# Channel layers over row blocks of 512, 64+448, 448 and 128+128, and 256 and 320, with left rows carried to the next pass

## The chip, the cores and the metric

One NeuronCore of one Trainium2 chip runs the whole program. The metric is device time in microseconds of one execution; the median of three runs stands for the kernel.

## What is computed

Four batches of 576 tokens with 512 channels go through three layers:

- attention over 8 heads of 64, where scores below the row's maximum minus tau are dropped before the softmax;
- a mixing layer and the channel layers: `u = x + h` (h mixes the tokens through a rank of 32), then `u + relu(u @ w_ch1) @ w_ch2`, with 512 to 2048 to 512 channels and the same weights for every token;
- a mixture of 8 experts: a gate gives each token an expert (a local gate can keep the expert of the token before), and the token goes through that expert's two layers of 512 to 1024 to 512.

The channel layers treat each token (each row) by itself: any rows can share a pass over the weights.

## The kernel before

Activations are kept transposed: a tile `yT` holds 128 channels on the partitions, four such groups `d`, and the 576 rows of a batch along the free dimension. `X[b]` is that tile for batch b; two tiles alternate, so batch b+2 takes the tile of batch b.

The channel layers keep the precision of float32 by splitting each operand into a high and a low part (tiles ending in h and l) and adding three products: high by high, high by low, low by high. Each product is a matmul of TensorE, with a 128 by 128 block of weights held in the array and the rows as the moving operand.

- `mix(b)` (L583) splits the rows of batch b into `uh` and `ul`: ScalarE copies (L591), VectorE subtracts (L592), in 8 steps.
- `load_w(b, f)` (L598) fetches one of 16 slices f of both weight matrices from DRAM and splits it.
- `mlp_l1(b, f)` (L618) makes the hidden values of slice f. It goes over the rows in two blocks, `HALVES`, of 256 and 320. For each block twelve matmuls (L628 to L630, over four k) add up in one bank of PSUM; ScalarE takes the relu from it (L631), VectorE the low part (L632).
- `mlp_l2(b, f0)` (L636) multiplies four slices of hidden values by the second weights, again twelve matmuls for a block of rows and a group d (L645 to L647); VectorE adds the bank to `yT` (L648).
- `channel(b)` (L651) runs 16 slices of layer 1 and three of the four rounds of layer 2; `channel_end(b)` (L662) the last round and `logits(b)`: the gate's matmuls (L675), a copy (L676), six transposes (L683) and two reductions (L684).
- `store_rows(b)` (L688) transposes the rows back and writes them to DRAM; `route(b)` (L701) works out each token's expert and its rank among that expert's tokens with many small VectorE instructions and four small matmuls, one of them L737.

The PSUM banks of the channel layers come from `mm_tile` (L137), which has two. Attention has its own: two tiles for scores (`s`, L132) and two banks for transposes (`tp`). A score tile is filled by L293 and L295, read by VectorE for the maximum (L328), by ScalarE for the exponential (L339) and by VectorE for the mask (L343). The probabilities are transposed (L390), copied out (L391, L398) and multiplied by v (L409, L410, L413); a chain per head pair then normalises and mixes them, ending in L467.

The order of the work comes from `interleave` (L72), which takes the next piece of whichever generator is least far along; the second number of each pair is the total of the costs that its generator reports, and every block of the channel layers reports 1.5. A scheduler of the language then orders each engine's instructions by that order and by what is ready; it does not change the program's pieces. Attention of batch 0 runs alone with the conversion of the weights beside it. After it (L785) the attention of batch b runs beside the channel layers of batch b-1:

```python
    for b in range(1, B):
        interleave((attention(b), 65.0), (channel(b - 1), 82.0), (STORE.get(b - 2, iter(())), 15.0),
                   (route(b - 2), 5.0) if b > 1 else ((1.0 for _ in conv), 30.0))
        if b == 1:
            cvs.close()
        interleave((mix(b), 2.1), (channel_end(b - 1), 18.0))
        STORE[b - 1] = store_rows(b - 1)
```

The channel layers of the last batch run at L1183 beside `early_slots()` (L915): the stored rows and the routing of batch 2, then slots of two experts' first tokens (their indices are cast at L911), and the loads of the first expert's weights. The experts follow; their first rows are gathered at L1059. Their layer 1 is L1106 to L1108, their layer 2 L1151 to L1153, there with 512 columns of weights as the moving operand.

Of the kernel before, what the change touches and what calls it, by code (L numbers as in the profile page):

```python
# [8 lines left out]
F32 = mybir.dt.float32  # L9
# [21 lines left out]
CH = 96  # L31
# [52 lines left out]
def attention_channel_moe(ctx, tc, qk, vv, tau, umat, vrep, wch, wgl, wexp, consts, out):  # L84
# [52 lines left out]
    def mm_tile(name):  # L137

        NM[0] += 1
        if PX and TURN[0] and NM[0] % 3 == 0:  # L140
            return PX[0].tile([128, 512], F32, tag="l1", name=name, bufs=2)
        return MM[0].tile([128, 512], F32, tag="mm", name=name, bufs=2)
# [437 lines left out]
        while pend or CHAIN:  # L580
            piece()

    def mix(b):  # L583

        u = X[b]
        uh = mlp.tile([128, 4, S], F32R, tag="uh", name=f"uh{b}")
        ul = mlp.tile([128, 4, S], F32R, tag="ul", name=f"ul{b}")
        for o, n in HALVES:
            c = slice(o, o + n)
            for d in range(4):  # L590
                act.activation(uh[:, d, c], u[:, d, c], AF.Copy)  # L591
                dve.tensor_tensor(out=ul[:, d, c], in0=u[:, d, c], in1=uh[:, d, c].bitcast(F32), op=ALU.subtract)  # L592
                yield 0.15
        U[b] = (uh, ul, u)

    W, LAST = {}, []

# [17 lines left out]
            r.append((hi, lo))  # L615
        W[nm] = r

    def mlp_l1(b, f, hs):  # L618
        uh, ul, _ = U[b]
        (w1h, w1l), _ = W[f"{b}_{f}"]  # L620
        hh = mlp.tile([128, S], F32R, tag="hh", name=f"hh{b}_{f}", bufs=5)
        hl = mlp.tile([128, S], F32R, tag="hl", name=f"hl{b}_{f}", bufs=5)
        hs[f] = (hh, hl)
        for o, n in HALVES:
            pm = mm_tile(f"l1_{b}_{f}_{o}")[:, :n]
# [5 lines left out]
            act.activation(hh[:, o:o + n], pm, AF.Relu)  # L631
            dve.scalar_tensor_tensor(out=hl[:, o:o + n], in0=pm, scalar=0.0, in1=hh[:, o:o + n].bitcast(F32),  # L632
                                     op0=ALU.max, op1=ALU.subtract)
            yield 1.5

    def mlp_l2(b, f0, hs):  # L636
        yT = U[b][2]
        for d in range(4):
            wd = slice(d * 128, d * 128 + 128)
            for o, n in HALVES:  # L640
                pm = mm_tile(f"l2_{b}_{f0}_{d}_{o}")[:, :n]
                for f in range(f0, f0 + 4):
                    _, (w2h, w2l) = W[f"{b}_{f}"]
                    hh, hl = hs[f]
                    pe.matmul(pm, lhsT=w2h[:, wd], rhs=hh[:, o:o + n], start=(f == f0), stop=False)  # L645
                    pe.matmul(pm, lhsT=w2h[:, wd], rhs=hl[:, o:o + n], start=False, stop=False)  # L646
                    pe.matmul(pm, lhsT=w2l[:, wd], rhs=hh[:, o:o + n], start=False, stop=(f == f0 + 3))  # L647
                dve.tensor_tensor(out=yT[:, d, o:o + n], in0=pm, in1=yT[:, d, o:o + n], op=ALU.add)  # L648
                yield 1.5

    def channel(b):  # L651
        hs = {}
        load_w(b, 0)
        load_w(b, 1)
        for f in range(NF):
            yield from mlp_l1(b, f, hs)
            if f % 4 == 0 and f:
                yield from mlp_l2(b, f - 4, hs)
            load_w(b, f + 2)
        HS[b] = hs  # L660

    def channel_end(b):  # L662
        yield from mlp_l2(b, NF - 4, HS[b])
        yield from logits(b)

    HS, LG = {}, {}

    def logits(b):

        yT = U[b][2]  # L670
        lt = mlp.tile([128, S], F32, tag="yr", name=f"lt{b}", bufs=2)
        for o, n in HALVES:
            pl = mm_tile(f"lt{b}_{o}")
            for d in range(4):
                pe.matmul(pl[32 * d:32 * d + 32, :n], lhsT=wg_sb[:, d], rhs=yT[:, d, o:o + n], start=True, stop=True)  # L675
# [3 lines left out]
        L = LG[b] = mlp.tile([CH, NJ, 9], F32, tag="L", name=f"L{b}")  # L679
# [6 lines left out]
        yield 2.6  # L686

    def store_rows(b):  # L688

        yT = U[b][2]  # L690
        for c0 in range(0, S, 128):
            n = min(128, S - c0)
            py = px_tile("l2", f"py{b}_{c0}") if b == B - 2 else mm_tile(f"py{b}_{c0}")
            for d in range(4):
                pe.transpose(py[:n, d * 128:d * 128 + 128], yT[:, d, c0:c0 + n], ident)
            yr = mlp.tile([128, S], F32, tag="yr", name=f"yr{b}_{c0}", bufs=2)[:n, :DM]
            act.activation(yr, py[:n], AF.Copy)  # L697
            sp.dma_start(out=ydram[b * S + c0:b * S + c0 + n, :], in_=yr)
            yield 0.45

    def route(b):  # L701

        w = mlp
        rt_tile = (lambda n: px_tile("l1", n)) if b == B - 2 else mm_tile
# [482 lines left out]
    for _ in store_rows(B - 1):  # L1187
        pass
    for _ in route(B - 1):
        pass  # L1190
# [96 lines left out]
```

## Time and profile before

| what | value |
|---|---|
| median of 3 runs | 1058.18 us (1057.45 to 1060.41) |
| the profiled execution's own time | 1055.3 us |
| its span, from the first to the last instruction | 1053.5 us |
| mean granted clock of TensorE | 0.994 of full speed |

The profile is of one execution. Busy time of an engine is the time in which it has an instruction running; matmuls overlap in the records, so their start-to-start distances, not their durations, say what one costs. A few matmul records are missing. Engines are PE (TensorE's matmuls), PEld (its weight loads), DVE (VectorE), ACT (ScalarE), POOL (GpSimd) and SP (the queue of most transfers); a row of the windows gives the busy times in that order, POOL last, then the granted clock (PEclk), the DMA share and GB/s. A wait is idle time of an engine with what ended it. Stages are cut at the gate's matmuls (L675) that follow each batch's channel layers.

### The profile page before, as it was taken

The page shows a single profiled execution, that of the slowest core. Times are in us where ns is not written, and L with a number is a line of the kernel's source. Part 1 is how long each engine was busy: PE and PEld are TensorE (multiplying, and loading weights), DVE is VectorE, ACT ScalarE, POOL GpSimd, SP SyncE. Part 2 cuts the span into 40 slices and gives each one's busy share as a digit, 9 for nine tenths or more (in the row PEclk, how much of TensorE's full clock was granted, in tenths as well). Part 3 has the DMA queues.
Part 4 walks back from the last instruction along what each step waited for, and adds up shares of the span by engine and source line. Part 5 has one row for each costly group of instructions (what it writes and reads, how often), then busy time and mean ns, then how long its engine had stood idle before and what let it go on. Part 6 is the DMA issues. An engine that isn't in the chain of part 4 may idle for free. (4 is left out here: it accounts for less than half of the span.)

```text
span 1053.5 us, 19168 instructions
## 1 busy us (share of the span) xinstructions
PE 1014.9 (96%) x7083; PEld 897.4 (85%) x7084; DVE 706.6 (67%) x1709; ACT 570.2 (54%) x1216; POOL 134.6 (13%) x115
## 2 busy tenths in 40 slices
PE   7898999999999999999999999999999999999996
PEld 4666688898888999898989988999998988989984
DVE  7998676775777577576667655583367855566673
ACT  6888665674646466473646545432254344455462
POOL 1331132230100000000000000002420321111100
PEclk9999999999999999999999999999999999999998
DMA  6655577773423232141322101353145475456650
GB/s 213 217 155 153 151 227 237 246 228 108 133 70 104 66 101 86 57 132 57 105 77 66 51 31 61 112 194 107 54 151 180 151 265 170 150 187 208 204 180 15
DMA packets 59205, 143.80 MB, mean 136 GB/s; under 512 B 8349, under 2 KB 9117, under 8 KB 59104
## 3 DMA queue, kind: packets, MB, share of 16 engines
q1 hardware_dynamic: 55744, 132.28, 39.4%
q0 software_dynamic: 3360, 10.23, 3.0%
q8 instruction: 57, 0.93, 0.4%
q14 instruction: 44, 0.36, 0.1%
HBM read 124.65 MB, written 18.61 MB: 136 GB/s over the span
## 5 line engine op out<-in xcount | busy, mean ns | idle before, releaser
L628 PE MATMUL l<-uh,w0h 128*128 128x256 f32 (+1 forms) x512 | 159.1, 311 | 0.6 <-DVE L L684 0.2
L645 PE MATMUL l<-hh,w1h 128*128 128x256 f32 (+1 forms) x512 | 155.6, 304 | 0.0
L630 PE MATMUL l<-uh,w0l 128*128 128x256 f32 (+1 forms) x512 | 153.0, 299 | 0.0
L647 PE MATMUL l<-hh,w1l 128*128 128x256 f32 (+1 forms) x512 | 152.8, 299 | 0.0
L646 PE MATMUL l<-hl,w1h 128*128 128x256 f32 (+1 forms) x512 | 152.7, 298 | 0.0
L629 PE MATMUL l<-ul,w0h 128*128 128x256 f32 (+1 forms) x512 | 152.6, 298 | 0.0
L1037 ACT ACTIVATE eh<-ew 128x512 fp32r<-128x512 f32 x160 | 94.3, 628 | 71.8 <-PE el L1153 45.3
L1038 DVE TENSOR_TENSOR el<-ew,eh 128x512 fp32r<-128x512 f32 x160 | 106.7, 693 | 37.7 <-ACT eh L1037 36.3
L339 ACT ACTIVATE p<-s,st 128x576 f32<-128x576 f32 x144 | 104.5, 740 | 47.0 <-DVE st L328 46.2
L343 DVE SCALAR_TENSOR_TENSOR p<-s,st,p 128x576 f32<-128x576 f32 x144 | 114.2, 814 | 9.8 <-ACT p L339 6.2
L328 DVE TENSOR_REDUCE st<-s 128x1 f32<-128x576 f32 x144 | 105.1, 750 | 19.7 <-PE s L295 19.1
L391 ACT ACTIVATE ptt<-tp 128x512 f32<-128x512 f32 (+1 forms) x192 | 89.9, 495 | 41.2 <-PE tp L390 40.6
L648 DVE TENSOR_TENSOR yT<-l,yT 128x256 f32<-128x256 f32 (+1 forms) x128 | 58.3, 456 | 67.8 <-PE l L647 67.5
L293 PE MATMUL s<-kh,qs 128*128 128x288 f32 x320 | 95.1, 317 | 8.8 <-DVE p L343 6.8
L612 POOL TENSOR_TENSOR w1l<-wr,w1h 128x512 fp32r<-128x512 f32 x24 | 32.7, 1379 | 545.1 <-ACT w1h L610 534.3
L628 PEld LDWEIGHTS l<-uh,w0h 128*128 128x128 f32 x512 | 97.1, 190 | 4.3 <-ACT yr L697 1.7
L645 PEld LDWEIGHTS l<-hh,w1h 128*128 128x128 f32 x512 | 97.0, 189 | 2.5 <-DVE p L343 0.8
L390 PE MATMUL tp<-cst,p 128*128 128x128 f32 x576 | 90.0, 275 | 8.5 <-ACT ptt L391 8.2
L629 PEld LDWEIGHTS l<-ul,w0h 128*128 128x128 f32 x512 | 97.3, 190 | 0.5
L646 PEld LDWEIGHTS l<-hl,w1h 128*128 128x128 f32 x512 | 97.1, 190 | 0.6
L630 PEld LDWEIGHTS l<-uh,w0l 128*128 128x128 f32 x512 | 97.3, 190 | 0.1
L647 PEld LDWEIGHTS l<-hh,w1l 128*128 128x128 f32 x512 | 96.9, 189 | 0.2
(448 smaller groups left out, 2296.6 us busy)
## 6 DMA issues: line engine op xcount, KB each, us to landing
ew<-in_wexp_dram SPq DMA_DIRECT2D x80, 512.0 KB, 4.7
wr<-wdram SPq DMA_DIRECT2D x128, 256.0 KB, 2.9
cr<-in_wch_dram SPq DMA_DIRECT2D x32, 512.0 KB, 5.1
raw<-in_qk_dram SPq DMA_DIRECT2D x30, 304.0 KB, 3.2
wdram<-w SPq DMA_DIRECT2D x32, 256.0 KB, 2.8
v<-in_vv_dram SPq DMA_DIRECT2D x16, 352.0 KB, 3.6
raw<-in_qk_dram SPq DMA_DIRECT2D x16, 320.0 KB, 3.5
raw<-in_qk_dram SPq DMA_DIRECT2D x17, 288.0 KB, 3.5
```

What stands on the lines that cost most here:

```text
L293: pe.matmul(s["t"][:, h, :288], lhsT=qs[:, qc:qc + 128], rhs=kh[:, k0:k0 + 288], start=(j == 0), stop=False)
L328: dve.tensor_reduce(out=self.st[:, 0, h:h + 1], in_=self.t[h], axis=AX.XY, op=ALU.max, negate=True)
L339: act.activation(self.halves(h), self.t[h], AF.Exp, bias=self.st[:, 0, h:h + 1])
L343: dve.scalar_tensor_tensor(out=p, in0=self.t[h], scalar=self.st[:, 1, h:h + 1], in1=p, op0=ALU.is_ge, op1=ALU.mult, accum_out=self.rvs[:, ...
L628: pe.matmul(pm, lhsT=w1h[:, wk], rhs=uh[:, k, o:o + n], start=(k == 0), stop=False)
L629: pe.matmul(pm, lhsT=w1h[:, wk], rhs=ul[:, k, o:o + n], start=False, stop=False)
L630: pe.matmul(pm, lhsT=w1l[:, wk], rhs=uh[:, k, o:o + n], start=False, stop=(k == 3))
L645: pe.matmul(pm, lhsT=w2h[:, wd], rhs=hh[:, o:o + n], start=(f == f0), stop=False)
L646: pe.matmul(pm, lhsT=w2h[:, wd], rhs=hl[:, o:o + n], start=False, stop=False)
L647: pe.matmul(pm, lhsT=w2l[:, wd], rhs=hh[:, o:o + n], start=False, stop=(f == f0 + 3))
L1037: act.activation(hi, x, AF.Copy)
L1038: dve.tensor_tensor(out=lo, in0=x, in1=hi.bitcast(F32), op=ALU.subtract)
```

## The change

A pass p over the weights is no longer tied to one batch. Pass 0 takes rows 0 to 511 of batch 0. Pass 1 takes rows 0 to 447 of batch 1 together with the 64 left rows of batch 0, in one block of 512. Pass 2 takes rows 0 to 447 of batch 2 as one block, and the 128 left rows of batch 2 with the 128 left rows of batch 1 as a second block of 256. Pass 3 takes batch 3 in blocks of 256 and 320, as before. Left rows are copied to tiles `REST` before their tile is used again (one ScalarE copy each). Where a pass holds more than 576 rows, the surplus lies in a new pool `kx`, opened once the conversion's pool is closed.

The gate's matmuls for left rows come with the pass that holds them, so a batch's logits are complete one pass later for batches 0 and 1. Routing of batch 0 moves from beside attention of batch 2 to beside attention of batch 3, routing of batch 1 from there to `early_slots`. The stored rows of batches 0 and 1 are written in two parts. A block now reports 0.0055 per column in place of 1.5, and the totals given to `interleave` follow.

```diff
+OWN = (512, 448, S, S)
+def chunks_of(p):
+    if p == 0:
+        return ((512, ((0, 512, 0, 0),)),)
+    if p == 1:
+        return ((512, ((0, 448, 1, 0), (448, 64, 0, 512))),)
+    if p == 2:
+        return ((448, ((0, 448, 2, 0),)), (256, ((0, 128, 2, 448), (128, 128, 1, 448))))
+    return tuple((n, ((0, n, p, o),)) for o, n in HALVES)
+def pass_cost(p):
+    return 0.0055 * sum(n for n, _ in chunks_of(p))
...
+    REST, KX = {}, []
+    def rows_at(b, o, n, d):
+        if o >= OWN[b]:
+            return REST[b][:, d, o - OWN[b]:o - OWN[b] + n]
+        return X[b][:, d, o:o + n]
+    def mix(p):
...
+        if p in (1, 2):
+            b = p - 1
+            REST[b] = KX[0].tile([128, 4, S - OWN[b]], F32, name=f"rest{b}")
+            act.activation(REST[b], X[b][:, :, OWN[b]:], AF.Copy)
...
+        for (n, segs), (vh, vl) in zip(chunks_of(p), parts):
+            for a, m, b, o in segs:
+                for c in range(0, m, 256) if m > 320 else (0,):
+                    w = min(256, m - c) if m > 320 else m
+                    for d in range(4):
+                        x, y = rows_at(b, o + c, w, d), vh[d][:, a + c:a + c + w]
+                        act.activation(y, x, AF.Copy)
+                        dve.tensor_tensor(out=vl[d][:, a + c:a + c + w], in0=x, in1=y.bitcast(F32), op=ALU.subtract)
+                        yield 0.15
...
+    def mlp_l1(p, f, hs):
...
+        for i, ((n, _), (uh, ul)) in enumerate(zip(chunks_of(p), U[p])):
...
+            pm = mm_tile(f"l1_{p}_{f}_{i}")[:, :n]
             for k in range(4):
                 wk = slice(k * 128, k * 128 + 128)
-                pe.matmul(pm, lhsT=w1h[:, wk], rhs=uh[:, k, o:o + n], start=(k == 0), stop=False)
-                pe.matmul(pm, lhsT=w1h[:, wk], rhs=ul[:, k, o:o + n], start=False, stop=False)
-                pe.matmul(pm, lhsT=w1l[:, wk], rhs=uh[:, k, o:o + n], start=False, stop=(k == 3))
+                pe.matmul(pm, lhsT=w1h[:, wk], rhs=uh[k], start=(k == 0), stop=False)
+                pe.matmul(pm, lhsT=w1h[:, wk], rhs=ul[k], start=False, stop=False)
+                pe.matmul(pm, lhsT=w1l[:, wk], rhs=uh[k], start=False, stop=(k == 3))
+            act.activation(xh, pm, AF.Relu)
+            dve.scalar_tensor_tensor(out=xl, in0=pm, scalar=0.0, in1=xh.bitcast(F32), op0=ALU.max, op1=ALU.subtract)
+            yield 0.0055 * n
+    def mlp_l2(p, f0, hs):
...
+            for i, (n, segs) in enumerate(chunks_of(p)):
...
+                for a, m, b, o in segs:
+                    y = rows_at(b, o, m, d)
+                    dve.tensor_tensor(out=y, in0=pm[:, a:a + m], in1=y, op=ALU.add)
+                yield 0.0055 * n
...
+    def channel_end(p):
+        yield from mlp_l2(p, NF - 4, HS[p])
+        if p in (1, 2):
+            yield from logits(p - 1, OWN[p - 1], S)
+        yield from logits(p, 0, OWN[p])
+        if p == 2:
+            yield from store_rows(1, OWN[1], S)
+    def logits(b, t0, t1):
+        if t0 == 0:
+            LT[b] = KX[0].tile([128, S], F32, tag="lt", name=f"lt{b}", bufs=1) if OWN[b] < S else mlp.tile(
+                [128, S], F32, tag="yr", name=f"lt{b}", bufs=2)
...
+        yield 1.0
+        if t1 < S:
+            return
...
     for b in range(1, B):
-        interleave((attention(b), 65.0), (channel(b - 1), 82.0), (STORE.get(b - 2, iter(())), 15.0),
-                   (route(b - 2), 5.0) if b > 1 else ((1.0 for _ in conv), 30.0))
+        p = b - 1
+        beside = {1: [((1.0 for _ in conv), 30.0)], 2: [(STORE.get(0), 15.0)],
+                  3: [(STORE.get(1), 15.0), (store_rows(0, OWN[0], S), 0.5), (route(0), 5.0)]}[b]
+        interleave((attention(b), 65.0), (channel(p), 28 * pass_cost(p)), *beside)
         if b == 1:
             cvs.close()
-        interleave((mix(b), 2.1), (channel_end(b - 1), 18.0))
-        STORE[b - 1] = store_rows(b - 1)
+            KX.append(kxs.enter_context(tc.tile_pool(name="kx", bufs=1, side="right")))
+        interleave((mix(b), 2.1), (channel_end(p), 4 * pass_cost(p) + 6.0))
+        STORE[p] = store_rows(p, 0, OWN[p])
+    kxs.close()
...
     def early_slots():
         yield from STORE[B - 2]
+        yield from route(B - 3)
         yield from route(B - 2)
...
-    interleave((channel(B - 1), 82.0), (early_slots(), 27.0))
+    interleave((channel(B - 1), 28 * pass_cost(B - 1)), (early_slots(), 30.0))
```

## Rows read from the trace of the kernel before

**Rows 1.** The page: span and TensorE (busy us, share of the span, instructions).
```profile
span 1053.5 us, 19168 instructions
...
PE 1014.9 (96%) x7083; PEld 897.4 (85%) x7084; DVE 706.6 (67%) x1709; ACT 570.2 (54%) x1216; POOL 134.6 (13%) x115
```

**Rows 2.** Windows by stage, cut at L675: length, busy us (instructions) by engine, clock, DMA share, GB/s.
```profile
117.77:298.98 181.21, 174.51 (x1314) 157.94 (x1313) 123.76 (x263) 112.36 (x242) 41.47 (x31) 1.00 0.59 186
298.98:484.20 185.22, 183.72 (x1393) 165.92 (x1392) 129.25 (x319) 104.13 (x230) 0.00 (x0) 1.00 0.29 88
484.20:670.70 186.50, 183.79 (x1382) 166.13 (x1381) 122.19 (x309) 98.28 (x220) 0.00 (x0) 0.99 0.21 65
670.70:783.00 112.30, 112.30 (x859) 110.26 (x858) 58.07 (x196) 38.78 (x81) 27.20 (x21) 1.00 0.38 128
```

**Rows 3.** TensorE's waits in stage 1 (us in total, times, longest).
```profile
PE tp L390 <- ACT ptt L391: 2.7, 3, 1.2
PE s L293 <- DVE p L343: 1.9, 2, 1.0
PE po L409 <- ACT ptt L398: 1.2, 3, 0.5
```

**Rows 4.** TensorE's waits in stage 2, the longest.
```profile
PE row L737 <- DVE seq L735: 0.7, 1, 0.7
```

**Rows 5.** Timeline of TensorE late in stage 1 (start us, us); twelve matmuls between rows.
```profile
289.29 0.28 PE L645 MATMUL l<-hh,w1h 128*128 128x256 f32 x1
...
290.72 0.31 PE L645 MATMUL l<-hh,w1h 128*128 128x320 f32 x1
...
292.48 0.28 PE L645 MATMUL l<-hh,w1h 128*128 128x256 f32 x1
```

**Rows 6.** Timeline of TensorE in the expert layers; 34 and 43 matmuls between rows.
```profile
802.66 0.34 PE L1108 MATMUL el<-y0h,el 128*128 128x384 f32 x1
...
808.56 0.39 PE L1152 MATMUL el<-el,h_0h 128*128 128x512 f32 x1
...
818.40 0.39 PE L1153 MATMUL el<-eh,h_4l 128*128 128x512 f32 x1
```

**Rows 7.** TensorE groups by line and shape: xcount | busy us, mean ns | idle before.
```profile
L628 PE MATMUL l<-uh,w0h 128*128 128x320 f32 x256 | 82.6, 323 | 0.1
...
L628 PE MATMUL l<-uh,w0h 128*128 128x256 f32 x256 | 76.5, 299 | 0.5 <-DVE L L684 0.2
```

**Rows 8.** ScalarE groups by line and shape, layer 1.
```profile
L631 ACT ACTIVATE hh<-l 128x320 fp32r<-128x320 f32 x64 | 27.3, 426 | 0.1
...
L631 ACT ACTIVATE hh<-l 128x256 fp32r<-128x256 f32 x64 | 24.8, 387 | 23.6 <-PE l L630 23.5
```

**Rows 9.** VectorE groups by line and shape, channel layers and mix.
```profile
L648 DVE TENSOR_TENSOR yT<-l,yT 128x320 f32<-128x320 f32 x64 | 31.3, 488 | 35.3 <-PE l L647 35.2
L632 DVE SCALAR_TENSOR_TENSOR hl<-l,hh 128x320 fp32r<-128x320 f32 x64 | 31.1, 486 | 19.5 <-ACT hh L631 19.5
...
L648 DVE TENSOR_TENSOR yT<-l,yT 128x256 f32<-128x256 f32 x64 | 27.1, 423 | 32.5 <-PE l L647 32.3
L632 DVE SCALAR_TENSOR_TENSOR hl<-l,hh 128x256 fp32r<-128x256 f32 x64 | 27.0, 421 | 21.8 <-ACT hh L631 21.2
...
L592 DVE TENSOR_TENSOR ul<-yT,uh 128x320 fp32r<-128x320 f32 x16 | 7.1, 485 | 0.0
```

**Rows 10.** Timeline of TensorE at the end of stage 1.
```profile
287.31 0.39 PE L467 MATMUL pu<-vst,th 128*128 128x320 f32 x1
...
298.98 0.64 PE L675 MATMUL lt<-yT,wg_sb 128*32 128x256 f32 x8
299.55 0.40 PE L293 MATMUL s<-kh,qs 128*128 128x288 f32 x1
```

**Rows 11.** Line L911: duration ns min/median/max, first and last start us.
```profile
L911 DVE CAST idxa<-iia x1: 173/173/173, 714.1 to 714.1; 128x10 int32<-128x10 f32 x1
```

**Rows 12.** Line L1059, the early gathers, the same columns.
```profile
L1059 POOL DMA_INDIRECT yg<-ydram,idxa x5: 1002/1009/1178, 766.0 to 771.4; - x5
```

More of the change, by code (lines that the diff above doesn't have):

```diff
@@ L581, in attention_alone @@
             piece()
[L583 to L594, printed above, removed]
+    REST, KX = {}, []
[4 more added lines that the diff above has]
+    def mix(p):
+        uh = mlp.tile([128, 4, S], F32R, tag="uh", name=f"uh{p}")
+        ul = mlp.tile([128, 4, S], F32R, tag="ul", name=f"ul{p}")
+        if p in (1, 2):
+            b = p - 1
+            REST[b] = KX[0].tile([128, 4, S - OWN[b]], F32, name=f"rest{b}")
+            act.activation(REST[b], X[b][:, :, OWN[b]:], AF.Copy)
+        flat = [x.rearrange("q a b -> q (a b)") for x in (uh, ul)]
+        parts, used = [], 0
+        for n, segs in chunks_of(p):
+            if used + 4 * n <= 4 * S:
+                views = [[x[:, used + d * n:used + d * n + n] for d in range(4)] for x in flat]
+                used += 4 * n
+            else:
+                m = (4 * S - used) // n
+                over = [KX[0].tile([128, 4 - m, n], F32R, name=f"u{x}{p}b") for x in "hl"]
+                views = [[x[:, used + d * n:used + d * n + n] if d < m else y[:, d - m] for d in range(4)]
+                         for x, y in zip(flat, over)]
+            parts.append(views)
+        for (n, segs), (vh, vl) in zip(chunks_of(p), parts):
[7 more added lines that the diff above has]
+                        yield 0.15
+        U[p] = parts
     W, LAST = {}, []
@@ L616, in load_w @@
         W[nm] = r
[L618 to L625, printed above, removed]
+    def mlp_l1(p, f, hs):
+        (w1h, w1l), _ = W[f"{p}_{f}"]
+        hh = mlp.tile([128, S], F32R, tag="hh", name=f"hh{p}_{f}", bufs=5)
+        hl = mlp.tile([128, S], F32R, tag="hl", name=f"hl{p}_{f}", bufs=5)
+        hs[f], o = [], 0
+        for i, ((n, _), (uh, ul)) in enumerate(zip(chunks_of(p), U[p])):
+            if o + n <= S:
+                xh, xl = hh[:, o:o + n], hl[:, o:o + n]
+                o += n
+            else:
+                xh, xl = (KX[0].tile([128, n], F32R, tag=f"h{t}", name=f"h{t}{p}_{f}b", bufs=5) for t in "hl")
+            hs[f].append((xh, xl))
+            pm = mm_tile(f"l1_{p}_{f}_{i}")[:, :n]
@@ L638, in mlp_l2 @@
+    def mlp_l2(p, f0, hs):
         for d in range(4):
             wd = slice(d * 128, d * 128 + 128)
-            for o, n in HALVES:
-                pm = mm_tile(f"l2_{b}_{f0}_{d}_{o}")[:, :n]
+            for i, (n, segs) in enumerate(chunks_of(p)):
+                pm = mm_tile(f"l2_{p}_{f0}_{d}_{i}")[:, :n]
                 for f in range(f0, f0 + 4):
[L643 to L649, printed above, removed]
@@ L651, in channel @@
-    def channel(b):
+                    _, (w2h, w2l) = W[f"{p}_{f}"]
+                    xh, xl = hs[f][i]
+                    pe.matmul(pm, lhsT=w2h[:, wd], rhs=xh, start=(f == f0), stop=False)
+                    pe.matmul(pm, lhsT=w2h[:, wd], rhs=xl, start=False, stop=False)
+                    pe.matmul(pm, lhsT=w2l[:, wd], rhs=xh, start=False, stop=(f == f0 + 3))
+                for a, m, b, o in segs:
+                    y = rows_at(b, o, m, d)
+                    dve.tensor_tensor(out=y, in0=pm[:, a:a + m], in1=y, op=ALU.add)
@@ L652, in channel @@
+                yield 0.0055 * n
+    def channel(p):
         hs = {}
-        load_w(b, 0)
-        load_w(b, 1)
+        load_w(p, 0)
+        load_w(p, 1)
         for f in range(NF):
-            yield from mlp_l1(b, f, hs)
+            yield from mlp_l1(p, f, hs)
             if f % 4 == 0 and f:
[L658 to L672, printed above, removed]
+                yield from mlp_l2(p, f - 4, hs)
+            load_w(p, f + 2)
+        HS[p] = hs
+    def channel_end(p):
[5 more added lines that the diff above has]
+            yield from store_rows(1, OWN[1], S)
@@ L673, in logits @@
+    HS, LG, LT = {}, {}, {}
+    def logits(b, t0, t1):
+        if t0 == 0:
+            LT[b] = KX[0].tile([128, S], F32, tag="lt", name=f"lt{b}", bufs=1) if OWN[b] < S else mlp.tile(
+                [128, S], F32, tag="yr", name=f"lt{b}", bufs=2)
+        lt = LT[b]
+        for o, n in HALVES if t1 - t0 > 512 else ((t0, t1 - t0),):
             pl = mm_tile(f"lt{b}_{o}")
             for d in range(4):
-                pe.matmul(pl[32 * d:32 * d + 32, :n], lhsT=wg_sb[:, d], rhs=yT[:, d, o:o + n], start=True, stop=True)
+                pe.matmul(pl[32 * d:32 * d + 32, :n], lhsT=wg_sb[:, d], rhs=rows_at(b, o, n, d), start=True, stop=True)
@@ L676, in logits @@
             act.activation(lt[:, o:o + n], pl[:, :n], AF.Copy)
+        yield 1.0
+        if t1 < S:
+            return
         lt3 = lt.rearrange("q (p j) -> q j p", j=NJ)
-        L = LG[b] = mlp.tile([CH, NJ, 9], F32, tag="L", name=f"L{b}")
+        L = LG[b] = mlp.tile([CH, NJ, 9], F32, tag="L", name=f"L{b}", bufs=2)
         for j0 in range(0, NJ, 3):
@@ L685, in logits, with store_rows @@
                               axis=AX.X, op=ALU.add)
[L686 to L692, printed above, removed]
+        yield 1.0
+    def store_rows(b, t0, t1):
+        for c0 in range(t0, t1, 128):
+            n = min(128, t1 - c0)
             py = px_tile("l2", f"py{b}_{c0}") if b == B - 2 else mm_tile(f"py{b}_{c0}")
             for d in range(4):
-                pe.transpose(py[:n, d * 128:d * 128 + 128], yT[:, d, c0:c0 + n], ident)
+                pe.transpose(py[:n, d * 128:d * 128 + 128], rows_at(b, c0, n, d), ident)
             yr = mlp.tile([128, S], F32, tag="yr", name=f"yr{b}_{c0}", bufs=2)[:n, :DM]
@@ L703, in route @@
         w = mlp
-        rt_tile = (lambda n: px_tile("l1", n)) if b == B - 2 else mm_tile
+        rt_tile = (lambda n: px_tile("l1", n)) if b in (1, 2) else mm_tile
         c0, c1 = b * NJ, b * NJ + NJ
@@ L1186, in attention_channel_moe @@
         pass
-    for _ in store_rows(B - 1):
+    for _ in store_rows(B - 1, 0, S):
         pass
```

7 lines of the change are left out of this document (1 added, 6 removed).

## The prediction, made before the changed kernel was run

> **What bounds the kernel now.** I read the page first: the span of the profiled execution is 1053.5 us, and TensorE is busy for 96% of it [rows 1]. A busy TensorE is not a TensorE at its peak, so I then cut the span at the gate matmuls that end each pass of the channel layers (L675) and read four stages [rows 2]. Stages 1 to 3 run the channel layers of batches 0, 1 and 2 beside the attention of batches 1, 2 and 3, and take 181.2, 185.2 and 186.5 us. Stage 4, the channel layers of batch 3, takes 112.3 us. VectorE is busy for 58 to 70% of stages 1 to 3 once its busy time is divided by the stage (123.8 of 181.2, 129.3 of 185.2, 122.2 of 186.5), ScalarE for less, DMA for at most 0.59. TensorE runs at a granted clock of 0.99 to 1.00, which is the 2.4 GHz level. The waits of TensorE say the same: 5.8 us at the three longest in stage 1 [rows 3] and, as the longest, 0.7 us in stage 2 [rows 4]. So TensorE's own stream sets the time from 118 us on, and a change there is worth what it takes out of that stream.
>
> What one matmul costs the stream is the distance from its start to the next start. In the channel layers twelve matmuls of 256 columns run from 289.29 to 290.72 us, 119.2 ns each, and twelve of 320 columns from 290.72 to 292.48 us, 146.7 ns each [rows 5]. Sixty-four more columns cost 27.5 ns, 0.43 ns a column; at that rate 256 columns are 110 ns, and some 9 ns are left that every matmul pays whatever its width. The expert layers show wider ones: 34 of 384 columns from 802.66 to 808.56 us, 173.5 ns each, and 43 of 512 columns from there to 818.40 us, 228.8 ns each [rows 6]. They lie on the same line (119.2 + 256 x 0.43 = 229).
>
> **Part 1: fewer, wider matmuls.** Each of L628 to L630 and L645 to L647 runs 256 times with 256 columns and 256 times with 320 [rows 7], that is 64 times each in a pass; six lines make 384 pairs a pass, and a pair takes 119.2 + 146.7 = 265.9 ns, so a pass takes 102.1 us. After the change the columns of all passes together are the same 4 x 576 (512, 512, 704, 576).
> - Passes 0 and 1 have one matmul of 512 columns in place of each pair: 228.8 - 265.9 = -37.1 ns, times 384 = -14.2 us each.
> - Pass 2 has 448 and 256 columns. No row has 448; halfway between 384 and 512 is 201.2 ns. 201.2 + 119.2 - 265.9 = +54.5 ns, times 384 = +20.9 us.
> - Pass 3 is as before.
>
> The sum is -7.5 us, from 768 matmuls fewer. Bounds: the 512-column rows have the weights moving and the hidden values held, the channel layers the other way round, so the price is not shown for them. At one end there is no fixed part at all and nothing is saved (0 us). At the other the fixed part is twice what the line gives, 18 ns, which puts 512 columns at 220 ns and 448 at 195: 2 x 384 x -45.9 + 384 x 48.3 = -16.7 us. I take -7.5, as the channel layers' own two widths and the expert rows agree on the line.
>
> The Trainium skill (TensorE: Matmul & The Clock Gate, "Back-to-back issue gap") gives a warm gap of N/2.4 + 2.5 ns, which would put only 2.5 ns of fixed cost on a matmul. The trace disagrees at 256 columns: 119.2 ns against 109.2.
>
> **Part 2: emptying the banks.** A chunk's result is taken from PSUM by ScalarE (L631) and then VectorE (L632) in layer 1, by VectorE alone (L648) in layer 2. ScalarE takes 387 ns for 256 columns and 426 for 320 [rows 8], VectorE 421 and 486, and 423 and 488 [rows 9]. Drawn on, 512 columns take 0.54 + 0.68 = 1.22 us. There are two banks, so this must fit beside the next chunk: before, 0.91 us beside twelve 256-column matmuls (1.43 us); in passes 0 and 1, 1.22 us beside twelve of 512 (2.75 us), so it gets easier. In pass 2 it gets tighter: the 448-column chunk takes 0.50 + 0.62 = 1.12 us beside 1.43 us, and the spare falls from 0.52 to 0.31 us. If that were lost 32 times it would cost 32 x 0.21 = 6.7 us; I take 0, because 186.5 - 102.1 = 84.4 us of other matmuls lie between the 32 pairs of that stage and stretch the same room.
>
> VectorE's own load: stage 1 saves 3.6 us in L632 (16 x 0.68 for 32 pieces that took 14.5) and 3.7 in L648; 116.5 of 167 us is 70%, against 68% before. Stage 2 saves 3.6 and 1.1: 124.6 of about 170 is 73%, and less once the routing of batch 0 has left it. Stage 3 adds about 6.8 (L632 in two pieces, L648 in three): 129 of 208 is 62%. No engine becomes the bound by these.
>
> **Part 3: the seams between passes.** The splitting of the next pass's input (mix) has 12 steps before pass 1 and 16 before pass 2, for 8, and a copy of the carried rows. A step is below 0.49 us on VectorE [rows 9]. The last attention matmul of stage 1 starts at 287.31 us, the gate matmuls at 298.98 us [rows 10]: 11.7 us of channel work cover the old mix (8 steps, under 4 us). After the change that cover shrinks by four groups' saving (4 x 0.44 = 1.8 us) and the longer mix takes 2 to 4 us more, so 2 to 4 us of it remain. Cost 0; without the cover it would be the 4 us, twice. The gate matmuls keep their number, in other widths. The transposes of batch 0 now come at the end of stage 2, those of batches 1 and 2 both at the end of stage 3; the extra serial piece I price like the routing's wait, 0.7 us [rows 4].
>
> **Part 4: what is moved.** Routing batch 0 leaves stage 2 (taking its 0.7 us wait along) for stage 3; batch 1 leaves stage 3 for stage 4. It issues four small matmuls, some thirty small VectorE instructions, one ScalarE one and no DMA. In stage 4 it comes ahead of the early slots, whose indices were ready at 714.1 us [rows 11] while the gather that reads them started at 766.0 us [rows 12]: 52 us of slack hide it and what is queued behind it on VectorE; without that slack it would cost its length. The expert loads on SP, queued behind that routing, start later by as much. Two blocks of stored rows (four transposes, one ScalarE copy, one SP transfer each) come a stage later or at the seam; they are read first by that same gather. SP has nothing else added, and POOL nothing. What is left is the wait that stage 2 loses, -0.7 us, and the four matmuls in stage 4 with their copies, +0.5 us (an estimate from the gate matmuls, which hold the stream from 298.98 to 299.55 us [rows 10]).
>
> **Sum.** -7.5 for part 1, -0.7 for the wait that leaves stage 2, +0.7 for the seam and +0.5 for stage 4 = -7.0 us. By stage: 181.2 - 14.2 = 167.0; 185.2 - 14.2 - 0.7 = 170.3; 186.5 + 20.9 + 0.7 = 208.1; 112.3 + 0.5 = 112.8 us. The profiled execution took 1055.3 us, which becomes 1048.3. It lay 0.3% under the median of the three runs (1058.18), so the median becomes 1051.2 us. Some 0.3%, 3.2 us, is what a measurement can tell from no change.
>
> **Rivals.** *The fixed part is smaller for these matmuls.* Weights held and inputs moving, 512 columns could take longer than the expert rows' 228.8 ns. At 236 ns, with 206 for 448, the sum is -22.9 + 22.8: nothing is saved, and halfway there is -3.7 us. Against it stands that 256 and 320 columns of these very lines already show the 9 ns. A time of 1054.5 to 1058.2 us. By the skill's gap, named above, 768 matmuls would save 768 x 2.5 ns = 1.9 us. I give this 0.16.
>
> *Attention becomes the bound in stages 1 and 2 (slower).* Channel matmuls are what TensorE does while an attention step waits for VectorE and ScalarE. Stages 1 and 2 lose 14.2 us of that filling each, while stage 3 pays its 20.9 us in full. The place is the scores' two PSUM tiles, held until the masking L343, and the transposes' two banks, emptied by L391 [rows 3]. It decides once more than 7.5 of the 28.4 us, 26%, come back as waits; if 60% do, the time is +9.5 us, 1067.7; if 45% do, 1063.5. For it: stage 1 already waits 5.8 us at these places. Against it: VectorE's share hardly rises, and the attention of batch 0, with no channel work beside it, is over when stage 1 begins at 117.77 us [rows 2], far below 167 us. I give 0.14.
>
> *Coarser pieces also save waits.* With 28 pieces beside attention in place of 56, TensorE changes over less, and the roomier banks could end the 5.8 us of stage 1: up to -12.8 us, 1045.4 us. Against it: a changeover has no cost of its own in a row that I found. I give 0.10.
>
> **How the numbers follow.** My forecast, 1047 to 1055 us, has 0.60. Faster by over 0.3% comes from it (0.58), from the third rival and a little of the first: 0.71. Within 0.3%: 0.16. Slower: 0.13, from the second rival. The range 1045 to 1060 us holds the forecast, the first rival, the third's upper part and the start of the second; the bank term of pass 2 (+6.7) also ends inside it.
>
> **What would show it.** Right: matmuls of 512 columns in the channel layers that start 227 to 231 ns apart, of 448 about 201; 384 fewer in each of passes 0 and 1 and as many as now in passes 2 and 3; stages of about 167, 170, 208 and 113 us; TensorE's waits in stages 1 and 2 still below 8 us together. Wrong: spacing of 236 ns or more (first rival); waits at L293 and L390 that grow past 7 us in stages 1 and 2 (second); a wait of L628 for L632 in stage 3 (pass 2's banks); a gap at a seam; a gather that starts late in stage 4.

## The result and the profile after

The changed kernel took 1050.12 us (median of 4 runs, 1048.89 to 1050.66) against 1058.72 us (4 runs, 1057.45 to 1060.41) of the kernel before on the same chip: a ratio of 0.9916, interval 0.9899 to 0.9933, or 8.9 us less (7.1 to 10.7). The profiled execution took 1050.24 us.

The page of the changed kernel, as [rows 1]:
```profile
span 1048.5 us, 17636 instructions
...
PE 1011.2 (96%) x6315; PEld 845.4 (81%) x6316; DVE 707.3 (67%) x1689; ACT 569.1 (54%) x1198; POOL 133.5 (13%) x115
```
TensorE has 7083 - 6315 = 768 matmuls fewer and still 96% of the span.

The stages of the changed kernel, with the columns of [rows 2]. The gate matmuls are now at L730. Here a stage is cut at the first of them after its last channel matmul; in the rows of the experiments the cuts are rounded and lie up to 0.4 us ahead of it.
```profile
117.70:285.59 167.89, 161.50 (x929) 124.40 (x929) 118.56 (x238) 112.45 (x234) 41.16 (x31) 1.00 0.62 200
285.59:452.49 166.90, 166.82 (x978) 129.78 (x977) 122.31 (x274) 100.94 (x215) 0.00 (x0) 1.00 0.30 96
452.49:657.97 205.48, 204.75 (x1387) 179.52 (x1386) 129.39 (x324) 100.27 (x220) 0.00 (x0) 1.00 0.18 58
657.97:774.44 116.47, 116.44 (x885) 112.78 (x884) 64.73 (x230) 39.28 (x85) 26.73 (x21) 1.00 0.37 126
```
Against [rows 2] stage 1 is 13.3 us shorter, stage 2 18.3 us, stage 3 19.0 us longer, stage 4 4.2 us longer. The sum is 656.7 us against 665.2, 8.5 us less, close to the whole gain. Batch 1's gate and transposes for its left rows now lie after the cut between stages 3 and 4; the gate of batch 2's own rows starts at 660.7 us. Cut there, stage 4 is 113.7 us.

TensorE's waits in the changed kernel (us in total, times, longest), the three longest of stage 1, then stage 3; stage 2 shows none.
```profile
PE s L311 <- DVE p L361: 2.6, 3, 1.5
PE tp L408 <- ACT ptt L409: 1.7, 2, 1.1
PE po L427 <- ACT ptt L416: 0.8, 1, 0.8
...
PE lg L741 <- ACT lt L731: 0.3, 1, 0.3
PE s L311 <- DVE p L361: 0.2, 1, 0.2
```
They answer to [rows 3, 4]. The three rows of stage 1 make 5.1 us (before 5.8), with the smaller ones 6.0 (before 6.3), and the 0.7 us of the routing in stage 2 is gone. No row names the banks (a channel matmul for L681).

TensorE's timeline in the changed kernel (start us, us), as [rows 5]: 24 matmuls of 512 columns lie between the first two rows, 12 of 448 between the third and fourth, 12 of 256 between the fourth and fifth.
```profile
279.38 0.39 PE L692 MATMUL l<-hh,w1h 128*128 128x512 f32 x1
...
284.82 0.39 PE L692 MATMUL l<-hh,w1h 128*128 128x512 f32 x1
...
646.24 0.36 PE L692 MATMUL l<-hh,w1h 128*128 128x448 f32 x1
...
648.70 0.28 PE L692 MATMUL l<-hh_12b,w1h 128*128 128x256 f32 x1
...
650.13 0.37 PE L692 MATMUL l<-hh,w1h 128*128 128x448 f32 x1
```
5.44 us / 24 = 226.7 ns for 512 columns, 2.46 / 12 = 205 ns for 448, 1.43 / 12 = 119.2 ns for 256.

The groups that empty the banks in the changed kernel (xcount, busy us, mean ns, idle before), as [rows 8, 9]:
```profile
L680 ACT ACTIVATE hh<-l 128x512 fp32r<-128x512 f32 x32 | 18.7, 583 | 0.0
L680 ACT ACTIVATE hh<-l 128x448 fp32r<-128x448 f32 x16 | 8.7, 543 | 17.6 <-PE l L679 17.6
...
L681 DVE SCALAR_TENSOR_TENSOR hl<-l,hh 128x512 fp32r<-128x512 f32 x32 | 21.9, 686 | 7.8 <-ACT hh L680 7.7
...
L681 DVE SCALAR_TENSOR_TENSOR hl<-l,hh 128x448 fp32r<-128x448 f32 x16 | 10.0, 623 | 11.4 <-ACT hh L680 11.1
```
448 columns take 0.54 + 0.62 = 1.17 us, below the 1.43 us of the twelve 256-column matmuls beside them.

The indices and the early gather in the changed kernel (ns min/median/max, first and last start us), as [rows 11, 12]:
```profile
L1122 POOL DMA_INDIRECT yg<-ydram,idxa x5: 994/1006/1180, 756.8 to 762.2; - x5
...
L973 DVE CAST idxa<-iia x1: 157/157/157, 709.6 to 709.6; 128x10 int32<-128x10 f32 x1
```
The slack between them is 47 us, where it was 52.

One thing in this trace is not the change's. After stage 4 its tail is 274.06 us, where before it was 1053.5 - 783.0 = 270.5. ScalarE's and TensorE's timelines in the expert layers of the changed kernel (in brackets: idle before, and what ended it):
```profile
829.22 0.62 ACT L1100 ACTIVATE eh<-ew 128x512 fp32r<-128x512 f32 x1
833.38 0.38 ACT L1173 ACTIVATE h_5h<-el 128x256 fp32r<-128x256 f32 x1 [3.53 <-remote]
...
834.28 0.38 PE L1169 MATMUL el<-y1h,eh 128*128 128x256 f32 x1 [2.62 <-DVE h_5l L1174]
```
ScalarE sat idle for 3.5 us, and TensorE for 2.6 us behind it. Matmuls of 512 columns then start 0.43 us apart from 836.38 to 838.08 us, at a granted clock of 0.50, the 1.2 GHz level. A second trace of the same kernel (below) has nothing of it.

### The profile page after: what moved, and what is told of

It is laid out like the page before. It is cut to its first block, busy times and chain, and to the rows that moved or that the text cites. A ratio compares the mean times of both kernels' runs of the same rounds, so it can differ in the third digit from the quotient of the medians.

```text
span 1048.5 us, 17636 instructions
## 1 busy us (share of the span) xinstructions
PE 1011.2 (96%) x6315; PEld 845.4 (81%) x6316; DVE 707.3 (67%) x1689; ACT 569.1 (54%) x1198; POOL 133.5 (13%) x115
## 5 line engine op out<-in xcount | busy, mean ns | idle before, releaser
L677 PE MATMUL l<-uh,w0h 128*128 128x256 f32 (+2 forms) x352 | 125.7, 357 | 0.0
L679 PE MATMUL l<-uh,w0l 128*128 128x256 f32 (+2 forms) x352 | 121.5, 345 | 0.6 <-POOL w0l L656 0.6
L678 PE MATMUL l<-ul,w0h 128*128 128x256 f32 (+2 forms) x352 | 121.5, 345 | 0.0
L692 PE MATMUL l<-hh,w1h 128*128 128x512 f32 (+3 forms) x320 | 115.7, 361 | 0.0
L693 PE MATMUL l<-hl,w1h 128*128 128x512 f32 (+3 forms) x320 | 114.0, 356 | 0.0
L694 PE MATMUL l<-hh,w1l 128*128 128x512 f32 (+3 forms) x320 | 112.3, 351 | 0.0
L313 PE MATMUL s<-kl,qs 128*128 128x288 f32 x320 | 90.3, 301 | 0.0
L408 PEld LDWEIGHTS tp<-cst,p 128*128 128x128 f32 x576 | 68.7, 141 | 22.7 <-ACT ptt L409 16.6
L311 PEld LDWEIGHTS s<-kh,qs 128*128 128x128 f32 x320 | 61.3, 192 | 18.4 <-issue 7.2
L427 PE MATMUL po<-ptt,v 128*64 128x256 f32 (+1 forms) x256 | 70.0, 413 | 1.7 <-ACT ptt L415 0.9
L681 DVE SCALAR_TENSOR_TENSOR hl<-l,hh 128x512 fp32r<-128x512 f32 (+2 forms) x80 | 46.4, 580 | 37.4 <-ACT hh L680 37.0
```

Source lines behind the costliest of these rows:

```text
L311: pe.matmul(s["t"][:, h, :288], lhsT=qs[:, qc:qc + 128], rhs=kh[:, k0:k0 + 288], start=(j == 0), stop=False)
L408: pe.transpose(tp[:, c - c0], src[:, c * 128:c * 128 + 128], ident)
L677: pe.matmul(pm, lhsT=w1h[:, wk], rhs=uh[k], start=(k == 0), stop=False)
L678: pe.matmul(pm, lhsT=w1h[:, wk], rhs=ul[k], start=False, stop=False)
L679: pe.matmul(pm, lhsT=w1l[:, wk], rhs=uh[k], start=False, stop=(k == 3))
L692: pe.matmul(pm, lhsT=w2h[:, wd], rhs=xh, start=(f == f0), stop=False)
```

## The experiments

Ratios are to the kernel before on the same chip.

**The change again, and the change with narrow blocks.** The second kernel carries the same rows in the same way, but splits the 512-column blocks of passes 0 and 1 in two. What differs is the width and, with it, the number of pieces: a narrow block hands over to the attention twice as often.
```diff
-        return ((512, ((0, 512, 0, 0),)),)
+        return ((256, ((0, 256, 0, 0),)), (256, ((0, 256, 0, 256),)))
...
-        return ((512, ((0, 448, 1, 0), (448, 64, 0, 512))),)
+        return ((256, ((0, 256, 1, 0),)), (256, ((0, 192, 1, 256), (192, 64, 0, 512))))
```


> The change, unedited, for a second trace. Both theories expect 1050 us (1049 to 1051). In the first trace of the change the expert stage lost 3.6 us against before: ScalarE idle for 3.5 us at 829.8 us and TensorE for 2.6 us behind it, then a few us at half clock. If the place of the instructions in the program causes this, the same wait (ScalarE before the relu of h_5 in the second expert unit) stands in this trace again; if it is an accident of one execution, it is gone and the span is 3 to 4 us shorter.

> The change with passes 0 and 1 in two blocks of 256 each in place of one of 512; rows carried, work moved and costs reported as in the change. As many matmuls as before the change (3072). Theory (a fixed 9 ns per matmul on a full TensorE stream): passes 0 and 1 take 384 x (2 x 119.2 - 228.8) = 3.7 us more each than in the change, and pass 2 still pays its 20.9 us over before, so 1050.1 + 7.4 = 1057.5 us, the time of before within 1.5 us. Rival (the gain comes from the carried rows, the moved routing and stores or the other order, not from the widths): 1050 us.

The change took 1046.24 us, ratio 0.9915 (0.9895 to 0.9936), with a span of 1045.6 us. The kernel with narrow blocks took 1056.36 us, 1.0021 (1.0006 to 1.0037). Its stages 1 and 2:
```profile
118.00:290.70 172.70, 164.18 (x1312) 148.26 (x1312) 121.11 (x268) 113.45 (x249) 42.74 (x31) 1.00 0.62 195
290.70:462.30 171.60, 170.55 (x1362) 153.60 (x1361) 125.26 (x306) 102.11 (x232) 0.00 (x0) 1.00 0.30 94
```
and those of the second trace of the change:
```profile
118.60:286.67 168.07, 161.69 (x929) 124.51 (x928) 117.17 (x237) 112.06 (x233) 40.94 (x31) 1.00 0.63 200
286.67:453.70 167.03, 166.97 (x980) 129.81 (x980) 122.41 (x274) 101.06 (x215) 0.00 (x0) 1.00 0.31 96
```
Width is worth 4.6 us in each of the two stages and nothing elsewhere: 8.2 us by the spans (1053.8 to 1045.6), 10.1 by the medians. The price line makes it 2 x 384 x (2 x 119.2 - 228.8) = 7.4 us, and the 226.7 ns measured make it 9.0. The greater number of pieces hardly explains the loss, as finer pieces took time off in the last experiment. Carrying rows without wider blocks gains nothing.

**The moved routing alone.** The kernel before, with routing of batch 0 beside attention of batch 3 and that of batch 1 in the early slots; blocks and rows as before.
```diff
-        L = LG[b] = mlp.tile([CH, NJ, 9], F32, tag="L", name=f"L{b}")
+        L = LG[b] = mlp.tile([CH, NJ, 9], F32, tag="L", name=f"L{b}", bufs=2)
...
-                   (route(b - 2), 5.0) if b > 1 else ((1.0 for _ in conv), 30.0))
+        beside = {1: [((1.0 for _ in conv), 30.0)], 2: [], 3: [(route(0), 5.0)]}[b]
...
+        yield from route(B - 3)
...
-    interleave((channel(B - 1), 82.0), (early_slots(), 27.0))
+    interleave((channel(B - 1), 82.0), (early_slots(), 30.0))
```
(A line left out here gives the routing of batch 1 the PSUM tile that the routing of batch 2 uses.)

> The kernel before with only the routing moved as in the change (batch 0 to beside attention of batch 3, batch 1 into the early slots). Theory: 0 to -1 us against before (the 0.7 us wait of the routing in stage 2 and nothing else), so 1058 us. Rival (the moved work brings the gain): 1050 to 1054 us.

It took 1050.55 us, 0.996 (0.9943 to 0.9977): 4.2 us less, where my theory had 0 to 1. Its stages 2 to 4:
```profile
300.90:483.10 182.20, 181.74 (x1385) 165.07 (x1383) 127.62 (x302) 103.97 (x230) 0.00 (x0) 1.00 0.29 89
483.10:665.90 182.80, 181.73 (x1383) 164.55 (x1382) 122.51 (x309) 98.37 (x221) 0.00 (x0) 1.00 0.21 66
665.90:780.30 114.40, 114.18 (x864) 111.09 (x862) 62.05 (x212) 38.48 (x81) 26.38 (x21) 1.00 0.38 126
```
Against [rows 2], stage 2 loses 3.0 us and stage 4 pays 2.1. But stage 3 also loses 3.7 us, and it has a routing beside it as before, only of an older batch. (Some 1.3 us of this belong to the one trace of the kernel before: from 495.1 to 498.5 us TensorE ran at a granted clock of 0.51, its 1.2 GHz level. Two later traces of kernels that route at the same place have no such stretch and show that stage as 185.2 and 185.3 us, so 2.4 is the safe figure.) So what the routing costs in stage 3 is not its work but when it comes.

**Three kernels on why.** The first only gives the kernel before the second buffer for `L`, a control for the other thing that the last kernel changed.

> The kernel before with one more buffer for the logits tile L, as in the change and in the run that moved only the routing; every engine has the same instructions in the same order as before. A control: if only the routing's move brought the 4 us of that run, this one takes the time of before (ratio 1.000 within 0.002). If the shifted addresses brought them: ratio 0.996.

It took 1053.13 us, 1.0006 (0.9992 to 1.0019): the buffer does nothing. The second spreads the routing over more of the stage:
```diff
-                   (route(b - 2), 5.0) if b > 1 else ((1.0 for _ in conv), 30.0))
+                   (route(b - 2), 1.6) if b > 1 else ((1.0 for _ in conv), 30.0))
```


> The kernel before with the routing of batches 0 and 1 spread over its whole stage (weight 1.6 in place of 5.0, so its three bursts start at 0, 40 and 80% of the stage instead of 0, 12 and 24%). Nothing is moved to another stage. Theory (the 4 us of the moved routing come from attention steps that wait in the first part of stages 2 and 3 behind the routing's bursts on VectorE): stages 2 and 3 are 2 to 3 us shorter each, 1054 us. Rival (they come from the routing no longer needing logits that have just been made): no change, 1058 us within 1.5.

It took 1051.84 us, 0.9998 (0.9985 to 1.0011). Spreading alone brings nothing; the first piece is still issued at the head of the stage. The third leaves the weight and delays that first piece, in the function `route`:
```diff
+        if b < B - 2:
+            yield 0.6
```


> The kernel before with the routing of batches 0 and 1 kept in its stage but begun at 12% of it instead of at its start (an empty first piece). Theory (the 4 us of the moved routing come from its first burst, which stands at the head of stages 2 and 3 on logits just made and holds VectorE and TensorE there): stages 2 and 3 are 2 to 3 us shorter each, the time is that of the run that moved the routing, ratio 0.996. Rival (it takes leaving the stage, or older logits): ratio 1.000 within 0.0015.

It took 1050.86 us, 0.9954 (0.9934 to 0.9974), as much as the moved routing brought. Its stages 2 and 3:
```profile
296.50:480.10 183.60, 183.14 (x1393) 165.81 (x1392) 129.40 (x319) 104.20 (x231) 0.00 (x0) 1.00 0.28 88
480.10:662.60 182.50, 181.76 (x1383) 164.47 (x1382) 122.39 (x309) 98.49 (x221) 0.00 (x0) 1.00 0.21 66
```
The longest wait of TensorE in stage 3 of the kernel before:
```profile
PE s L293 <- DVE p L343: 1.7, 1, 1.7
```
With the moved routing that row shows 0.3 us, and with the delayed one it is gone, as is the 0.7 us of [rows 4]. Waits name 2.4 us of the 4.2 to 4.9. TensorE's timeline shows where more of it lies. At the head of stage 2 in the kernel before:
```profile
305.66 0.29 PE L295 MATMUL s<-kl,qs 128*128 128x288 f32 x1
305.79 1.03 PE L390 MATMUL tp<-cst,p 128*128 128x128 f32 x8
307.08 0.33 PE L390 MATMUL tp<-cst,p 128*128 128x128 f32 x1 [0.25 <-ACT ptt L391]
308.10 0.33 PE L737 MATMUL row<-cst,seq 96*1 96x96 f32 x2 [0.69 <-DVE seq L735]
308.35 0.41 PE L628 MATMUL l<-uh,w0h 128*128 128x320 f32 x1
```
and with the delayed routing, twelve channel matmuls from the second row to just before the third:
```profile
303.55 0.29 PE L295 MATMUL s<-kl,qs 128*128 128x288 f32 x1
303.68 0.31 PE L628 MATMUL l<-uh,w0h 128*128 128x320 f32 x1
...
305.43 0.60 PE L695 MATMUL py<-cst,yT 128*128 128x128 f32 x4
305.86 0.93 PE L390 MATMUL tp<-cst,p 128*128 128x128 f32 x7
306.55 0.38 PE L293 MATMUL s<-kh,qs 128*128 128x288 f32 x1
```
In the kernel before, the transposes follow the scores at once, and the routing's first matmul (L737) stands ahead of the next channel block. Nine transposes and the two matmuls of L737 take 2.56 us from 305.79 us on; with the delayed routing a channel block comes first, and seven transposes take 0.69 us, 0.1 each. So about 1.4 us are lost there. In stage 3 nine transposes take 3.27 us in the kernel before (490.65 to 493.92), of which some 2.4 are lost: 3.8 us in all. The cost is thus where the routing's first piece stands, a serial run of small VectorE steps on logits that have just been made, at the moment when the new attention starts. How much its steps on VectorE take and how much the other order of TensorE's matmuls, which comes with them, is not separated.

**The other way to cut pass 2.** The change with 512 + 192 columns in pass 2 in place of 448 + 256.
```diff
-        return ((448, ((0, 448, 2, 0),)), (256, ((0, 128, 2, 448), (128, 128, 1, 448))))
+        return ((512, ((0, 512, 2, 0),)), (192, ((0, 64, 2, 512), (64, 128, 1, 448))))
```


> The change with pass 2 in blocks of 512 and 192 in place of 448 and 256: the same number of matmuls and columns. Theory (straight line): a pair takes 228.8 + 91.7 = 320.5 ns against 323.2, so the time of the change less 1 us, 1049 us. Rival 1 (the banks set pass 2): the emptying of a 512 block takes 1.22 us and must fit beside 192 columns, 1.1 us, so 32 waits of 0.15 to 0.3 us, 1054 to 1060 us. Rival 2 (a narrow matmul has a floor of 109 ns, as the 56-column ones of the slots step): 384 x 17 ns = 6.6 us more, 1056 us.

It took 1065.85 us, 1.0103 (1.0077 to 1.013), 19.6 us more than the change. TensorE's timeline in its stage 3, ten matmuls of 192 columns between the rows:
```profile
667.59 0.28 PE L693 MATMUL l<-hl_12b,w1h 128*128 128x192 f32 x1
...
668.71 0.27 PE L694 MATMUL l<-hh_15b,w1l 128*128 128x192 f32 x1
```
and its longest waits in that stage:
```profile
PE tx L452 <- ACT yT L434: 2.2, 6, 0.7
PE py L752 <- DVE rv L370: 1.6, 1, 1.6
PE po L427 <- ACT ptt L416: 1.5, 2, 1.1
```
A step of 192 columns is 1.12 / 10 = 112 ns, where the line gives 9 + 192 x 0.43 = 92. By 512 + 192 a pair costs 226.7 + 112 = 338.7 ns against 205 + 119.2 = 324.2, times 384 = 5.6 us. The stage grew by 223.1 - 205.5 = 17.6 us. Its waits rose from 0.5 to 9.8 us, which with the 5.6 leaves 3 open. Emptying 512 columns takes 0.58 + 0.69 = 1.27 us, and twelve matmuls of 192 give it 1.34 us. The rows name attention steps that wait for ScalarE and VectorE, none the banks. The next kernel, with 512 + 64 columns, has as thin a spare in every pass (1.28 us beside 1.34), yet its stage 3 has 1.5 us of waits and is 212.4 - 185.2 = 27.2 us longer than that of before, where its blocks alone make 28.0. So the thin spare by itself does not bring such waits; what brings them here is open.

**Why rows are carried at all.** The kernel before with blocks of 512 + 64 columns in every pass, and no carry; and with three blocks of 192.
```diff
+MH = ((0, 512), (512, 64))
...
-        for o, n in HALVES:
+        for o, n in MH:
...
-            yield 1.5
+            yield 3.0 * n / S
```
(the loops of the mix and of both layers; the kernel with thirds has 192 at 0, 192 and 384 there.)

> The kernel before with the channel layers of every batch in blocks of 512 and 64 in place of 256 and 320: no rows are carried, the number of matmuls is that of before. Theory (straight line, 9 ns + 0.43 ns a column): a pair takes 228.8 + 36.7 = 265.5 ns against 265.9, the time of before, 1058 us. Rival (a matmul with new weights cannot follow the one before sooner than about 109 ns, as the 56-column ones of the slots step): 228.8 + 109 = 338 ns a pair, 4 x 384 x 72 = 110 us more, 1169 us.

> The kernel before with three blocks of 192 rows per batch in place of 256 and 320: the same columns in 1536 matmuls more. Theory (9 ns fixed): 3 x 91.7 - 265.9 = 9.2 ns for each of 4 x 384, +14.1 us, 1073 us. With 2.5 ns fixed: +3.8 us, 1062.5 us. With a floor of 109 ns a matmul: 327 ns for the three, +94 us, 1153 us.

512 + 64 took 1168.78 us, 1.1036 (1.1005 to 1.1067). TensorE's timeline, ten matmuls of 64 columns between the rows:
```profile
321.53 0.28 PE L647 MATMUL l<-hl,w1h 128*128 128x64 f32 x1
...
322.65 0.28 PE L648 MATMUL l<-hh,w1l 128*128 128x64 f32 x1
```
64 columns cost 112 ns, as much as 192. The kernel before had this floor already: the narrow matmuls of the slots (L880, 10 and 56 columns) start 109 to 112 ns apart. A pass then costs 384 x (226.7 + 112 - 265.9) = 28.0 us more and four passes 112 us, where 110 were measured. The Trainium skill (TensorE: Matmul & The Clock Gate, "LDWEIGHTS (loading the stationary operand)") gives a weight load of 128 columns as 128 / 1.2 = 107 ns; the trace, in which each of these matmuls has a weight load, is close to that as a floor. That the weight load sets the floor is argued, not shown: no run leaves it out. By the straight line this kernel, with as many matmuls as before, would only have equalled the time of before. Fewer matmuls need carried rows, and the floor makes the narrow block a loss.

Thirds took 1278.92 us, 1.2076 (1.2034 to 1.2117), at a mean clock of 0.955. The floor explains 4 x 384 x (3 x 112 - 265.9) = 108 of the 220 us. TensorE's waits explain some 75 more: they come to 102 us, where the kernel before has 27. The transposes L391 waited 37.3 us for L392 alone, and channel matmuls waited 20.8 us for VectorE to empty their banks (L633, L649), although emptying 192 columns takes only 0.33 + 0.35 us beside 1.34. Some 37 us are left. TensorE also ran in many stretches at its 1.2 GHz level, the longest from 873 to 897 us (granted clock 0.50); how much that took is not separated.

**Finer pieces.** The change as it is, but a block hands over to the attention in mid-block: every block over 400 columns in halves (run twice), then every block in quarters. The quarters, in both layers:
```diff
+                if k < 3:
+                    yield 0.001375 * n
...
-            yield 0.0055 * n
+            yield 0.001375 * n
...
+                    if f < f0 + 3:
+                        yield 0.001375 * n
...
-                yield 0.0055 * n
+                yield 0.001375 * n
```


> The change with blocks of 448 and 512 columns reported in two halves (six matmuls each), so attention pieces can stand between the halves. The work is the same. Theory: what the change left as waits is in stage 1 (6.1 us by TensorE's waits, at the transposes and scores); finer pieces give back up to 3 us of it, 1043 to 1046 us. Rival (the scheduler already places attention by what is ready, whatever the pieces): the time of the change, 1046 to 1050 us, ratio to before 0.9915.

> The change with its wide blocks reported in halves, once more, for the interval: ratio 0.989 to before if the 2.4 us over the change are real, 0.9915 if they were the chip's.

> The change with every block of the channel layers reported in four pieces of three matmuls. Theory (finer pieces let attention start sooner): at or below the run with halves, ratio 0.986 to 0.989. Rival (more changes between attention and channel work cost as much as the waits they save): 0.990 to 0.993.

Halves took 1042.02 us, 0.9892 (0.9873 to 0.991), and 1041.64 us, 0.9858 (0.9837 to 0.988); quarters 1040.48 us, 0.985 (0.9827 to 0.9873). Halves and quarters can't be told apart. The quarters beat both kernels: 15.8 us under the kernel before by the ratio, and, by 0.985 / 0.9915, some 7 us under the change, which didn't run beside them (5.8 by the medians on one chip). Their stages 1 to 4:
```profile
117.40:283.00 165.60, 160.33 (x928) 123.09 (x928) 115.78 (x236) 111.76 (x233) 41.17 (x31) 1.00 0.64 197
283.00:449.60 166.60, 166.29 (x978) 128.49 (x977) 122.45 (x274) 101.06 (x216) 0.00 (x0) 1.00 0.31 96
449.60:655.10 205.50, 204.97 (x1388) 178.53 (x1387) 129.60 (x325) 101.77 (x220) 0.00 (x0) 1.00 0.18 58
655.10:771.30 116.20, 116.14 (x886) 112.86 (x885) 64.38 (x229) 39.49 (x84) 26.23 (x21) 1.00 0.37 127
```
Cut at the gates themselves the four stages make 654.2 us against 657.0 in the second trace of the change, and 2.2 of these 2.8 us are in stage 1. Stage 1 varies by about as much between traces in which it is the same (part 3 below), so where the gain of the ratio lies is not shown.

## Why the prediction was right, and where its steps were not

The side was right, and so was the size: 7.0 us forecast, 8.9 measured (7.1 to 10.7), 1051.2 us against 1050.1. The main term was right for its reason; that the whole came so close is in part luck, as two smaller terms were both too small and partly offset each other. By stage 167.0, 170.3, 208.1 and 112.8 us were forecast; cut at the gates of the batch's own rows, as the forecast's stages were, they are 167.9, 169.9, 205.2 and 113.7.

**Part 1** held. 512 columns cost 226.7 ns (228.8 forecast), 448 cost 205 (201.2), 256 still 119.2. With these the sum is 2 x 384 x (226.7 - 265.9) + 384 x (205 + 119.2 - 265.9) = -30.1 + 22.4 = -7.7 us, forecast -7.5. The pair with narrow blocks shows it as a time. The Trainium skill (TensorE: Matmul & The Clock Gate, "Back-to-back issue gap") gives N / 2.4 + 2.5 ns for a single, isolated matmul, which the prediction did not say; at 512 columns that is 216 ns. The trace of this stream lies above it at this width as it did at 256.

**Part 2**, the banks at nothing, held for 448 + 256: no wait names them, and emptying took 1.17 us of the 1.43 (1.12 forecast). With 512 + 64 even a spare of 0.06 us was enough. But the length of the emptying does not decide alone: with three blocks of 192 the banks were waited for, though emptying took half of the time beside it.

**Part 3** was too small. TensorE shows no wait for the mix at a seam. But between the moved routing alone and the change with narrow blocks stages 2 to 4 grow by 492.5 - 479.4 = 13.1 us, where 384 x (2 x 119.2 + 205 + 119.2 - 2 x 265.9) = 11.8 us come from the blocks: the carry, with the stores in two parts and the costs that the blocks report, cost 1.3 us there. By the medians (1056.36 - 1050.55 = 5.8 us, of which 384 x (4 x 119.2 + 205 + 119.2 - 3 x 265.9) = 1.3 from the blocks) it cost 4.5 us. Forecast was 0.7. Which of the two is nearer is open: stage 1 has the same work in the five traced kernels with the blocks of before and takes 179.3 to 184.0 us (the longest holds 3.4 us at the 1.2 GHz level).

**Part 4** is the step that failed: "What is left is the wait that stage 2 loses, -0.7 us, and the four matmuls in stage 4 with their copies, +0.5 us". Measured alone, it is -4.2 us (-2.4 to -6.0). By stage it is -3.0 us in stage 2 (forecast -0.7), -2.4 in stage 3 (forecast nothing) and +2.1 in stage 4 (forecast +0.5). I priced the wait that leaves stage 2 and missed the time that stands behind the transposes, and that stage 3 keeps a routing but not the moment at which it comes. The 52 us of slack did hold, 47 are left, but stage 4 still paid more than its four matmuls. With the terms as measured, -7.7 for the blocks, -4.2 for the routing and +1.3 to +4.5 for the carry, the sum is -10.6 to -7.4 us, which holds the 8.9.

**The rivals.** A smaller fixed part falls by the spacing. Attention as the bound falls by the waits, 6.0 us in stages 1 and 2 together, below the 8 that I had allowed. (VectorE's share, which I quoted against it as 58 to 70% of stages 1 to 3, is 66 to 70% by the numbers beside it; the argument doesn't change.) That coarser pieces save waits falls too: the waits of stage 1 stayed, and it was finer pieces that took time off.

## What to carry to other kernels

Price a matmul by its start-to-start distance, as a fixed part with a slope and a floor: here 9 ns + 0.43 ns a column, and no less than 112 ns; then choose row blocks so that none lies under the floor, if need be by carrying the remainder to the next pass. When work moves between stages, ask not only what it costs but what it meets at the moment it is issued: a delay of about an eighth of a stage brought 4.9 us here. And the width of a block and the piece after which it hands over are two choices: wide blocks in fine pieces were best.

## What was not expected of the hardware

- 64 and 192 columns cost the same 112 ns in a stream of matmuls with a weight load each, while 256 cost 119.2.
- Three blocks of 192 ran at a mean granted clock of 0.955, with many waits of TensorE, where the profiled executions of the other kernels had 0.992 to 0.998.
- One execution of the change had 3.5 us in which ScalarE stood idle before L1173, for a reason that the trace calls remote, and TensorE ran at its 1.2 GHz level after its own idle 2.6 us. It didn't come again in the second trace; its cause is open.
- In stage 3 of the kernel before TensorE fell to the 1.2 GHz level for 3.4 us soon after an idle of 1.65 us. Two later traces have the same idle (1.7 and 1.6 us) and stay at 2.4 GHz.
